# Block 0 of a fused retention and MLP kernel: who casts the first k and scales the first q, and which PSUM banks and which place four of its tiles have

## The chip, the cores and the metric

The kernel runs on one core of a Trainium2 chip. TensorE (PE) does the matrix products, VectorE (DVE), ScalarE (ACT) and GpSimd (POOL) the elementwise work, and SyncE (SP) issues most DMAs. The time is the device time of one execution in microseconds. The lower it is, the better.

## The reference, cut to what matters

```python
def _attn_ref(q, k, v):            # 4 batches, 8 heads, 768 steps, 64 wide
    gamma = 1.0 - 2.0 ** (-5.0 - np.arange(H))
    for t in range(S):
        state = gamma * state + outer(k[t], v[t])
        y[t] = scale * q[t] @ state

def _moe_ref(x, w_in, w_out):      # x: y as 3072 rows of 512; w_in 512 x 2048
    h = x @ w_in
    g = h * tanh(softplus(h))      # Mish
    return g @ w_out               # 2048 x 512
```

A decayed linear attention (retention) gives x, and a two-layer MLP with the Mish function follows. Inputs and output are float32.

## The kernel before

**Chunks and blocks.** The 24 chunks of 128 steps (6 for each batch) are worked off in blocks: block 0 holds four chunks (512 rows), the ten others two each. In a chunk the retention is a masked product of scores with v (the present part) plus q times a state of the chunks before (the past part). A block's y, transposed and rounded to fp16, is `xt`, the moving operand of the first MLP layer. Later blocks use Strassen-like seven products for both layers (`g1_seven`, `seven`); block 0 computes its first layer plainly, in 16 tiles u of 128 hidden features by 512 rows: `first_g1` for u = 0 to 3, in two halves of 256 rows (s = 0 for chunks 0 and 1, s = 1 for chunks 2 and 3), and `g1` for u = 4 to 15. Each tile is four matmuls over the 512 inputs (one half: four of 256 columns) and ends in `mish`, a ScalarE activation from PSUM.

**The order is written out.** The program states the order by hand, and each engine takes its instructions in that order; semaphores come from the data and the buffers. The function with the order of block 0 is `first_block`, followed by `first_g2` for the second layer.

**How block 0 starts.** `load_first_q` loads the q of all four chunks in two halves by heads, then k and v come in pairs of chunks (s = 0: chunks 0 and 1; s = 1: chunks 2 and 3), each in two halves of four heads (`load_two`), then the four slices of `w_in`, then those of `w_out`, all on SP's queue. `turn_first_q` scales one half of q to fp16 on VectorE (L255) and transposes it on PE (L261); `first_q_out` copies it out of PSUM. `cast_two` casts a half of k to fp16 on ScalarE (L286) or multiplies a half of v by its decay on GpSimd (L289); `turn_two` transposes k on PE (L300), and `turned_two` copies it out on ScalarE (L305). `scores_half` makes scores (L315), which VectorE masks in `mask_half` (L322). `outer_first` and `state_first` make the states (L334, L344, L346 on VectorE); `present_first` (L375) and `past_first` (L382) make y for two chunks in one PSUM tile, and `xt_out` copies both chunks to `xt` on ScalarE (L387). Here and there `spin` and `spin_wide` are matmuls on constants whose result nobody reads: they keep PE at work.

**Weights.** `cast_win` casts half a slice of `w_in` to fp16 (L212; L210 on ScalarE): slice 0 on GpSimd and VectorE, slices 1 and 2 on VectorE, slice 3 on ScalarE between two Mish. `cast_wout` does the same for `w_out` (L220 on VectorE, L223 on ScalarE). From these casts VectorE builds the sums for the later blocks (`win_sums`, L756; `weight_sums`, L708 to L711). In `first_g2`, PE's products (L1191) are copied out by ScalarE (L1197, and the snapshots L1200), then ScalarE casts its half of slice 2 of `w_out` (L223). GpSimd's `gate` (L428) makes it wait for `tmat`; behind it stand `cast_q` (L403) and `cast_v` (L420) of chunk 4, whose q and k PE then transposes in `turn` (L454).

**PSUM.** There are eight banks of 2 KB per partition. Pool `mmps` hands out four tiles of one bank in turn, pool `atps` two tiles of two banks in turn: scores, y, and later the outer products. A tile that is taken anew waits for the last reader of the tile that had its room.

Of the kernel before, what the change touches and what calls it, by code (L numbers as in the profile page):

```python
# [10 lines left out]
FP32 = mybir.dt.float32  # L11
AF = mybir.ActivationFunctionType
ALU = mybir.AluOpType
# [3 lines left out]
def kernel(  # L17
# [9 lines left out]
    nc = tc.nc  # L27
    B, H, S, D = q.shape
    d_model, d_ff = moe_w_in.shape
    P = 128  # L30
    C = 128
    NCH = S // C
    NCK = B * NCH
    HP = H // 2
    TB = 512
    CPB = TB // C
# [7 lines left out]
    FPS = NFB // NSL  # L44
# [10 lines left out]
    in_two = [vs_np[(jj % HB) * R + r] for r in range(R)]  # L55
    qvs_np = np.ascontiguousarray(np.concatenate([qs_np, vs_np, *spread, *in_two], 1))

    def toks(c):
        return slice(c * HB, (c + 1) * HB)
# [11 lines left out]
    op = ctx.enter_context(tc.tile_pool(name="rn_o", bufs=6))  # L71
# [10 lines left out]
    qs_spread = qvs[:, 2 * H:(2 + CPB) * H].rearrange("p (r h) -> p h r", r=CPB)  # L82
# [166 lines left out]
                q[0, a:a + H // 2, :TB].rearrange("h (p r) d -> p h r d", r=CPB))  # L249
        return qf  # L250

    def turn_first_q(qf, half):
        a, n = half * (H // 2), H // 2
        q16 = castp.tile([P, CPB, n, D], FP16, name="qfirst16", bufs=1, tag=f"qfirst16_{half}")
        nc.vector.tensor_tensor(  # L255
            q16.rearrange("p r h d -> p h r d"), qf[:, a:a + n],
            qs_spread[:, a:a + n].unsqueeze(3).broadcast_to((P, n, CPB, D)), op=ALU.mult)
        t_ps = mmps.tile([P, n // 2, CPB, P], FP16, name="t_ps", tag="mm")
        for i in range(n // 2):
            for r in range(CPB):  # L260
                nc.tensor.transpose(t_ps[:, i, r], q16[:, r, 2 * i:2 * i + 2], ident)  # L261
        return t_ps

    def first_q_out(half, t_ps, eng):
        n = HP // 2
        dst = qfirst_t[:, half * n:(half + 1) * n].rearrange("p i (t r) -> p i t r", r=CPB)
        src = t_ps.rearrange("p i r t -> p i t r")
        if eng is nc.scalar:
            nc.scalar.copy(dst, src)
        else:  # L270
            eng.tensor_copy(dst, src)
# [6 lines left out]
                "h (p r) d -> p h r d", r=R))  # L278
        raw[nm, s, half] = t

    def cast_two(nm, s, half):
        src = raw.pop((nm, s, half))
        if nm == "k":
            if s not in k16s:
                k16s[s] = castp.tile([P, 2, R, HP, D], FP16, name="qk16")
            nc.scalar.copy(k16s[s][:, half].rearrange("p r h d -> p h r d"), src)  # L286
        else:
            v16s[s, half] = castp.tile([P, R, HP, D], FP16, name="v16")
            nc.gpsimd.tensor_tensor(  # L289
                v16s[s, half].rearrange("p r h d -> p h r d"), src,  # L290
                vs_two[:, half * HP:(half + 1) * HP].unsqueeze(3).broadcast_to((P, HP, R, D)),
                op=ALU.mult)

    def turn_two(s, half):
        if s not in kts:
            kts[s] = qktp.tile([P, HP, R, P], FP16, name="qkt", bufs=4)
        t_ps = mmps.tile([P, HP // 2, R, P], FP16, name="t_ps", tag="mm")
        for j in range(HP // 2):
            for r in range(R):
                nc.tensor.transpose(t_ps[:, j, r], k16s[s][:, half, r, 2 * j:2 * j + 2], ident)  # L300
        t16s[s, half] = t_ps

    def turned_two(s, half):
        n = HP // 2
        nc.scalar.copy(kts[s][:, half * n:(half + 1) * n], t16s.pop((s, half)))  # L305
# [63 lines left out]
    def present_first(s, y, pairs):  # L369
        for i in pairs:  # L370
            half, j = divmod(i, HP // 2)
            for r in range(R):
                for c in range(2):
                    for hh in range(2):
                        nc.tensor.matmul(  # L375
                            y[64 * hh:64 * hh + 64, c, i], v16s[s, half][toks(c), r, 2 * j + hh],
                            amf[s, half][toks(c), hh, j, r], start=i == 0 and r == 0,
                            stop=s == 0 and c == 0 and r == R - 1, skip_group_check=True)

    def past_first(g, y):  # L380
        for i in range(HP):
            nc.tensor.matmul(  # L382
                y[:, g % 2, i], states[g - 1][:, i], qfirst_t[:, i, g * C:(g + 1) * C],
                start=False, stop=True, skip_group_check=True)

    def xt_out(g, y):
        nc.scalar.copy(xts[0][:, g:g + 2], y)  # L387

    def room16(g):
        if g not in cast:  # L390
# [54 lines left out]
    def spin_wide(at, n):  # L445
        nc.tensor.matmul(
            at[:, 0].rearrange("p j r t -> p (j r) t")[:, :n], tri,
            tri.unsqueeze(1).broadcast_to((P, n, C)), start=True, stop=True)
# [217 lines left out]
    def g1(blk, u):  # L666
        nt = BLOCKS[blk] * C
        per = TB // nt
        h_ps = mmps.tile([P, per, nt], FP32, name="h_ps", tag="mm")
        for j in range(per):  # L670
            s, f = divmod(u * per + j, FPS)
            for bp in range(NBP):
                nc.tensor.matmul(  # L673
                    h_ps[:, j], win(s, f, bp), xt(blk, bp),
                    start=(bp == 0), stop=(bp == NBP - 1))
        mish(blk, u, h_ps)
# [361 lines left out]
    def first_g1(h_ps, u, s):  # L1038
        t = slice(s * TB // 2, (s + 1) * TB // 2)
        for bp in range(NBP):  # L1040
            nc.tensor.matmul(  # L1041
                h_ps[:, 0, t], win(0, u, bp), xts[0][:, 2 * s:2 * s + 2, bp],
                start=bp == 0, stop=bp == NBP - 1, skip_group_check=True)

    def first_block():
# [11 lines left out]
        spin_wide(at, HP)  # L1057
        spin(at, 8)
        tq = turn_first_q(qf, 0)
        spin_wide(at, 3)  # L1060
        first_q_out(0, tq, nc.scalar)
        tq = [tq, turn_first_q(qf, 1)]
        cast_two("k", 0, 0)
        turn_two(0, 0)
        first_q_out(1, tq[1], nc.vector)
        turned_two(0, 0)
        cast_two("k", 0, 1)
        spin_wide(at, 3)
        scores_half(0, 0, at)
        mask_half(0, 0, at)  # L1070
        turn_two(0, 1)
        turned_two(0, 1)
        for half in range(2):
            cast_two("v", 0, half)
        at = at_tile()
        spin_wide(at, 3)
        scores_half(0, 1, at)
        mask_half(0, 1, at)
        cast_two("k", 1, 0)
# [6 lines left out]
        scores_half(1, 0, at)  # L1086
        mask_half(1, 0, at)
        y = atps.tile([P, 2, HP, C], FP32, name="y_ps", tag="at")
        present_first(0, y, range(HP))
        turn_two(1, 1)  # L1090
        turned_two(1, 1)
        state_first(1)
        past_first(1, y)
        xt_out(0, y)
        for half in range(2):
            cast_two("v", 1, half)
# [1 line left out]
        at = at_tile()  # L1098
        scores_half(1, 1, at)
        mask_half(1, 1, at)  # L1100
        y = atps.tile([P, 2, HP, C], FP32, name="y_ps", tag="at")
        outer_first(1, [0])
        state_first(2)
        h_ps = [mmps.tile([P, 1, TB], FP32, name="h_ps", tag="mm") for _ in range(2)]
        present_first(1, y, range(HP))
        past_first(2, y)
        past_first(3, y)
        xt_out(2, y)
        cast_win(0, 1, nc.vector)
        for u in range(FPS):  # L1110
            if u >= 2:
                h_ps.append(mmps.tile([P, 1, TB], FP32, name="h_ps", tag="mm"))
            first_g1(h_ps[u], u, 0)
        for u in range(FPS):
            first_g1(h_ps[u], u, 1)
# [280 lines left out]
```

## Time and profile before

| | |
|---|---|
| Runs before | 191.96, 193.19, 194.15 us; median 193.19 |
| Profiled execution | 192.43 us, its span 190.2 us |
| PE busy | 183.4 us, 96% of the span |
| VectorE, ScalarE, GpSimd busy | 155.3 us (82%), 127.7 (67%), 93.6 (49%) |
| Granted TensorE clock, mean | 0.997 |
| DMA | 36.17 MB, mean 190 GB/s |

A row of the trace in order of time reads: start in us from the span's start, us, engine, line, operation, output <- input, shapes, count, and in brackets how long the engine had been idle before it and what ended that wait. SPq and POOLq are issues of DMAs, PEld the loading of weights into PE. A row of the chain reads: start, us, engine, tile, line, count. A row of a stretch has its limits, its length, then for PE, PEld, DVE, ACT and POOL the busy us and the instructions, then the granted clock, the DMA's busy share and GB/s.

### The profile page before, as it was taken

Reading aid. Unit: us, or ns where it says so; the run is one execution under the profiler, and the core shown is the slowest. Engines: PE = TensorE matmul, PEld = TensorE weight load, DVE = VectorE, ACT = ScalarE, POOL = GpSimd, SP = SyncE. Lnnn points to the kernel's source line nnn. Section 1 sums busy time; section 2 is a strip of 40 time slices with the busy share of each in tenths; the row PEclk is TensorE's granted clock in tenths of the full one; section 3 lists DMA queues with packets and bytes.
Section 4 is the critical chain, followed back from the end, with each engine's and each line's share of the span. In section 5 each row is a group of like instructions: output and inputs, shape, how many; then the busy total and the mean of one; then the engine's idle time right before and its main releaser. Section 6 shows DMA issues by size and latency. Waiting matters only on the chain.

```text
span 190.2 us, 7745 instructions
## 1 busy us (share of the span) xinstructions
PE 183.4 (96%) x3298; PEld 156.1 (82%) x3298; DVE 155.3 (82%) x327; ACT 127.7 (67%) x246; POOL 93.6 (49%) x134
## 2 busy tenths in 40 slices
PE   6889999999999999999999999999999999999992
PEld 2457546885988988988988988988988989989981
DVE  3786799989899698797897897797897897796672
ACT  3564699463893893894794883883983974975960
POOL 6270206596777937933943934925925923000000
PEclk9999999999999999999999999999999999999998
DMA  5999999997999999999996996999997954300203
GB/s 164 351 369 406 404 408 259 293 263 77 193 190 264 197 258 245 158 207 173 139 206 160 173 164 193 192 116 172 177 177 152 142 163 60 114 3 6 107 0 110
DMA packets 95521, 36.17 MB, mean 190 GB/s; under 512 B 82560, under 2 KB 88960, under 8 KB 95488
## 3 DMA queue, kind: packets, MB, share of 16 engines
q1 hardware_dynamic: 74112, 32.78, 73.0%
q0 software_dynamic: 21088, 2.62, 21.6%
q8 instruction: 25, 0.41, 0.9%
q10 hardware_dynamic: 288, 0.30, 0.4%
q14 instruction: 8, 0.07, 0.1%
HBM read 27.30 MB, written 6.29 MB: 177 GB/s over the span
## 4 chain that ended last, share of the span: by engine, by line
PE 86%; DMA 5%; DVE 3%; ACT 1%; POOL 1%; issue 1%; DVEq 0%
PE o_ps L940 31%; PE h_ps L804 30%; PE h_ps L673 6%; PE o_ps L1191 5%; DMA qkt<-qk 3%; DMA qfirst<-in_q_dram 2%; PE o_ps L1251 2%; PE h_ps L1041 2%; PE y_ps L531 2%; PE at L498 2%; PE u_ps L484 2%; PE y_ps L542 1%; DVE am L322 1%; POOL qk L415 1%; DVE st L346 1%
## 5 line engine op out<-in xcount | busy, mean ns | idle before, releaser
L824 DVE TENSOR_TENSOR hsum<-h_ps,hsnap 128x512 f32<-128x512 f32 x60 | 38.7, 685 | 9.6 <-ACT hsnap L814 6.5
L814 ACT COPY hsnap<-h_ps 128x512 f32<-128x512 f32 x60 | 32.1, 589 | 9.9 <-PE h_ps L804 9.7
L804 PEld LDWEIGHTS <-wsum 128*128 128x128 f16 x640 | 36.2, 98 | 0.1
L819 ACT ACTIVATE g<-hsum 128x512 f16<-128x512 f32 x60 | 34.7, 642 | 0.5
L940 PEld LDWEIGHTS <-gsum 128*128 128x128 f16 x320 | 30.5, 98 | 3.7
L804 PE MATMUL h_ps<-xsum,wsum 128*128 128x128 f16 x480 | 30.1, 219 | 0.0
L940 PE MATMUL o_ps<-tmat,gsum 128*128 128x256 f16 x240 | 29.5, 273 | 0.0
L804 PEld LDWEIGHTS <-win 128*128 128x128 f16 x480 | 28.2, 98 | 0.9
L415 POOL DMA_DIRECT2D qk<-in_k_dram x36 | 27.6, 775 | 0.0
L940 PEld LDWEIGHTS <-g 128*128 128x128 f16 x248 | 22.7, 98 | 2.6
L403 POOL TENSOR_TENSOR qk<-qf,qvs 128x512 f16<-128x512 f32 x20 | 21.5, 1074 | 0.0
L420 POOL TENSOR_TENSOR v<-vf,qvs 128x512 f16<-128x512 f32 x20 | 21.1, 1077 | 0.0
L940 PE MATMUL o_ps<-wout,g 128*128 128x256 f16 (+1 forms) x168 | 20.8, 267 | 0.0
L804 PE MATMUL h_ps<-xt,win 128*128 128x128 f16 x320 | 19.6, 219 | 0.0
L549 ACT COPY hsum<-y_ps 128x512 f32<-128x512 f32 x9 | 5.3, 585 | 18.7 <-PE y_ps L542 16.3
L592 POOL TENSOR_TENSOR stc<-suc,gcv 128x256 f16<-128x256 f32 x15 | 9.9, 660 | 15.9 <-DVE suc L587 15.9
L961 DVE TENSOR_TENSOR osb<-o_ps,snap 128x256 f32<-128x256 f32 (+1 forms) x32 | 13.0, 413 | 4.8 <-PE o_ps L940 2.4
L949 ACT COPY snap<-o_ps 128x256 f32<-128x256 f32 x31 | 11.4, 371 | 5.5 <-PE o_ps L940 5.3
L428 POOL COPY gate<-gsum 128x1 f16<-128x1 f16 x10 | 1.9, 186 | 26.7 <-DVE gsum L911 26.7
L804 PE MATMUL h_ps<-xsum,win 128*128 128x128 f16 x160 | 12.3, 220 | 0.0
L804 PE MATMUL h_ps<-xt,wsum 128*128 128x128 f16 x160 | 12.2, 219 | 0.0
L819 ACT ACTIVATE g<-h_ps 128x512 f16<-128x512 f32 x20 | 12.0, 598 | 0.0
(138 smaller groups left out, 308.1 us busy)
## 6 DMA issues: line engine op xcount, KB each, us to landing
vf<-in_v_dram SPq DMA_DIRECT2D x24, 256.0 KB, 6.2
out_dram<-osb SPq DMA_DIRECT2D x22, 256.0 KB, 3.0
qf<-in_q_dram SPq DMA_DIRECT2D x20, 256.0 KB, 5.4
wi<-in_moe_w_in_dram SPq DMA_DIRECT2D x3, 1024.0 KB, 10.6
wt<-in_moe_w_out_dram SPq DMA_DIRECT2D x3, 1024.0 KB, 9.1
qk<-in_k_dram POOLq DMA_DIRECT2D x36, 64.0 KB, 4.7
qfirst<-in_q_dram SPq DMA_DIRECT2D x2, 512.0 KB, 4.3
kf<-in_k_dram SPq DMA_DIRECT2D x4, 256.0 KB, 5.0
```

Of the source, the lines that this page charges most:

```text
L403: nc.gpsimd.tensor_tensor(by_head(g, room16(g)[0]), by_head(0, loaded[g][0]), f.broadcast_to((P, 2, HP, D)), op=ALU.mult)
L415: nc.gpsimd.dma_start(room16(g)[1][:, x::2], src[:, HP * x:HP * x + HP])
L420: nc.gpsimd.tensor_tensor(room16(g)[2], loaded[g][2], vs.unsqueeze(2).broadcast_to((P, H, D)), op=ALU.mult)
L592: by.tensor_tensor(stcs[g], sus.pop(g), decay, op=ALU.mult)
L673: nc.tensor.matmul(h_ps[:, j], win(s, f, bp), xt(blk, bp), start=(bp == 0), stop=(bp == NBP - 1))
L804: nc.tensor.matmul(h_ps[g][:, f], w(g, f, d), x(d), start=first and f == 0 and d == 0, stop=d == n - 1, skip_group_check=True)
L814: nc.scalar.copy(x, h_ps)
L819: nc.scalar.activation(gt[:, fb:fb + FPS, j * P:(j + 1) * P], h, AF.Mish, scale=inv_boost3)
L824: nc.vector.tensor_tensor(h, h_ps, x, op=ALU.add)
L940: nc.tensor.matmul(t, x(f), w(f)[:, c], start=first and f == 0, stop=f == n - 1, skip_group_check=True)
L949: nc.scalar.copy(x[:, c], t)
L961: nc.vector.tensor_tensor(dst[:, c], t, plus[:, c], op=ALU.add)
```

## The change

1. `turn_first_q(qf, 1, True)`: of the second half of q, VectorE scales the first two heads and GpSimd the last two, a quarter of q.
2. The two halves of k of chunks 0 and 1 are cast by VectorE instead of ScalarE, right behind the scaling and ahead of the copy-out of q (`first_q_out(1)`); both are transposed and copied out before the first scores. On ScalarE two casts go, and the copies of both `kts` halves follow each other.
3. Three calls `spin_wide(at, 3)` become `spin_wide(at, 1)`.
4. y of chunks 2 and 3 is made in two `atps` tiles, of which each uses one bank, instead of one. `first_g1` of tiles 0 and 1 for s = 0 stands ahead of it.
5. `xt_out_by_two` copies chunk 2 on ScalarE and chunk 3 on VectorE, the latter behind `cast_win(0, 1)`.
6. `g1` of tiles 8 and 9 (`u // 2 == FPS`) takes its PSUM from `atps`, the pool of the scores, instead of `mmps`.

SP's order of instructions stays; GpSimd's order has one instruction more, ahead of the first v. PE has the same instructions apart from the width of three fillers.

```diff
--- before.py
+++ after.py
@@ -249,12 +249,15 @@
                 q[0, a:a + H // 2, :TB].rearrange("h (p r) d -> p h r d", r=CPB))
         return qf
 
-    def turn_first_q(qf, half):
+    def turn_first_q(qf, half, shared=False):
         a, n = half * (H // 2), H // 2
         q16 = castp.tile([P, CPB, n, D], FP16, name="qfirst16", bufs=1, tag=f"qfirst16_{half}")
-        nc.vector.tensor_tensor(
-            q16.rearrange("p r h d -> p h r d"), qf[:, a:a + n],
-            qs_spread[:, a:a + n].unsqueeze(3).broadcast_to((P, n, CPB, D)), op=ALU.mult)
+        m = n // 2 if shared else n
+        for b in range(0, n, m):
+            (nc.gpsimd if b else nc.vector).tensor_tensor(
+                q16[:, :, b:b + m].rearrange("p r h d -> p h r d"), qf[:, a + b:a + b + m],
+                qs_spread[:, a + b:a + b + m].unsqueeze(3).broadcast_to((P, m, CPB, D)),
+                op=ALU.mult)
         t_ps = mmps.tile([P, n // 2, CPB, P], FP16, name="t_ps", tag="mm")
         for i in range(n // 2):
             for r in range(CPB):
@@ -278,12 +281,16 @@
                 "h (p r) d -> p h r d", r=R))
         raw[nm, s, half] = t
 
-    def cast_two(nm, s, half):
+    def cast_two(nm, s, half, by_vector=False):
         src = raw.pop((nm, s, half))
         if nm == "k":
             if s not in k16s:
                 k16s[s] = castp.tile([P, 2, R, HP, D], FP16, name="qk16")
-            nc.scalar.copy(k16s[s][:, half].rearrange("p r h d -> p h r d"), src)
+            dst = k16s[s][:, half].rearrange("p r h d -> p h r d")
+            if by_vector:
+                nc.vector.tensor_copy(dst, src)
+            else:
+                nc.scalar.copy(dst, src)
         else:
             v16s[s, half] = castp.tile([P, R, HP, D], FP16, name="v16")
             nc.gpsimd.tensor_tensor(
@@ -373,18 +380,22 @@
                 for c in range(2):
                     for hh in range(2):
                         nc.tensor.matmul(
-                            y[64 * hh:64 * hh + 64, c, i], v16s[s, half][toks(c), r, 2 * j + hh],
+                            y[c][64 * hh:64 * hh + 64, i], v16s[s, half][toks(c), r, 2 * j + hh],
                             amf[s, half][toks(c), hh, j, r], start=i == 0 and r == 0,
                             stop=s == 0 and c == 0 and r == R - 1, skip_group_check=True)
 
     def past_first(g, y):
         for i in range(HP):
             nc.tensor.matmul(
-                y[:, g % 2, i], states[g - 1][:, i], qfirst_t[:, i, g * C:(g + 1) * C],
+                y[g % 2][:, i], states[g - 1][:, i], qfirst_t[:, i, g * C:(g + 1) * C],
                 start=False, stop=True, skip_group_check=True)
 
     def xt_out(g, y):
         nc.scalar.copy(xts[0][:, g:g + 2], y)
+
+    def xt_out_by_two(g, y):
+        nc.scalar.copy(xts[0][:, g], y[0])
+        nc.vector.tensor_copy(xts[0][:, g + 1], y[1])
 
     def room16(g):
         if g not in cast:
@@ -666,7 +677,10 @@
     def g1(blk, u):
         nt = BLOCKS[blk] * C
         per = TB // nt
-        h_ps = mmps.tile([P, per, nt], FP32, name="h_ps", tag="mm")
+        if u // 2 == FPS:
+            h_ps = atps.tile([P, 2, per, nt], FP32, name="h_ps", tag="at")[:, 0]
+        else:
+            h_ps = mmps.tile([P, per, nt], FP32, name="h_ps", tag="mm")
         for j in range(per):
             s, f = divmod(u * per + j, FPS)
             for bp in range(NBP):
@@ -1057,23 +1071,23 @@
         spin_wide(at, HP)
         spin(at, 8)
         tq = turn_first_q(qf, 0)
-        spin_wide(at, 3)
+        spin_wide(at, 1)
         first_q_out(0, tq, nc.scalar)
-        tq = [tq, turn_first_q(qf, 1)]
-        cast_two("k", 0, 0)
+        tq = [tq, turn_first_q(qf, 1, True)]
+        cast_two("k", 0, 0, True)
         turn_two(0, 0)
+        turned_two(0, 0)
+        cast_two("k", 0, 1, True)
+        turn_two(0, 1)
         first_q_out(1, tq[1], nc.vector)
-        turned_two(0, 0)
-        cast_two("k", 0, 1)
-        spin_wide(at, 3)
+        turned_two(0, 1)
+        spin_wide(at, 1)
         scores_half(0, 0, at)
         mask_half(0, 0, at)
-        turn_two(0, 1)
-        turned_two(0, 1)
         for half in range(2):
             cast_two("v", 0, half)
         at = at_tile()
-        spin_wide(at, 3)
+        spin_wide(at, 1)
         scores_half(0, 1, at)
         mask_half(0, 1, at)
         cast_two("k", 1, 0)
@@ -1086,11 +1100,12 @@
         scores_half(1, 0, at)
         mask_half(1, 0, at)
         y = atps.tile([P, 2, HP, C], FP32, name="y_ps", tag="at")
-        present_first(0, y, range(HP))
+        in_two = [y[:, c] for c in range(2)]
+        present_first(0, in_two, range(HP))
         turn_two(1, 1)
         turned_two(1, 1)
         state_first(1)
-        past_first(1, y)
+        past_first(1, in_two)
         xt_out(0, y)
         for half in range(2):
             cast_two("v", 1, half)
@@ -1098,18 +1113,19 @@
         at = at_tile()
         scores_half(1, 1, at)
         mask_half(1, 1, at)
-        y = atps.tile([P, 2, HP, C], FP32, name="y_ps", tag="at")
+        y = [atps.tile([P, 2, HP, C], FP32, name="y_ps", tag="at")[:, 0] for _ in range(2)]
         outer_first(1, [0])
         state_first(2)
         h_ps = [mmps.tile([P, 1, TB], FP32, name="h_ps", tag="mm") for _ in range(2)]
+        for u in range(2):
+            first_g1(h_ps[u], u, 0)
         present_first(1, y, range(HP))
         past_first(2, y)
         past_first(3, y)
-        xt_out(2, y)
         cast_win(0, 1, nc.vector)
-        for u in range(FPS):
-            if u >= 2:
-                h_ps.append(mmps.tile([P, 1, TB], FP32, name="h_ps", tag="mm"))
+        xt_out_by_two(2, y)
+        for u in range(2, FPS):
+            h_ps.append(mmps.tile([P, 1, TB], FP32, name="h_ps", tag="mm"))
             first_g1(h_ps[u], u, 0)
         for u in range(FPS):
             first_g1(h_ps[u], u, 1)
```

## The prediction

> **What bounds the kernel now.** I read the page first: one engine is busy nearly all the time.
>
> ```profile
> span 190.2 us, 7745 instructions
> PE 183.4 (96%) x3298; PEld 156.1 (82%) x3298; DVE 155.3 (82%) x327; ACT 127.7 (67%) x246; POOL 93.6 (49%) x134
> ```
>
> The profiled execution took 192.43 us, 2.2 more than its span, and the three runs have a median of 193.19 (191.96 to 194.15). PE is idle for 6.8 us in all. The stretches of equal work show where the idle time lies, and it is the stretch that the change edits:
>
> ```profile
> 0.00:17.00 17.00, 13.92 (x211) 7.88 (x212) 12.17 (x37) 7.83 (x12) 8.34 (x20) 1.00 0.95 312
> 17.00:31.00 14.00, 14.00 (x97) 7.90 (x95) 11.16 (x25) 11.28 (x19) 3.10 (x3) 1.00 1.07 396
> ```
>
> In the first 17 us PE is busy for 13.92 (3.08 idle, and part of the rest is `spin_wide`, which computes nothing); after it PE has no gap. The chain that ended last then stays on PE:
>
> ```profile
> 17.10 3.49 PE h_ps L1041 x32
> 20.59 0.37 PE u_ps L355 x16
> 20.96 10.53 PE h_ps L673 x48
> 31.50 6.11 PE o_ps L1191 x56
> ```
>
> Read alone, this says that whatever the prologue saves comes off the end. But a chain names one path. So I looked at what else could end at 37.5, in ScalarE's order of time and in the DMA of 3 to 31 us:
>
> ```profile
> DMA packets 10624, 10.75 MB, mean 384 GB/s; under 512 B 1486, under 2 KB 7552, under 8 KB 10621
> ...
> 18.73 1.30 DVE L212 CAST win<-wi 128x1024 f16<-128x1024 f32 x2 [1.48 <-DMA wi<-in_moe_w_in_dram]
> ...
> 24.00 1.04 ACT L210 CAST win<-wi 128x1024 f16<-128x1024 f32 x1 [0.57 <-DMA wi<-in_moe_w_in_dram]
> 24.95 0.59 ACT L689 ACTIVATE g<-h_ps 128x512 f16<-128x512 f32 x1
> 25.43 1.04 ACT L210 CAST win<-wi 128x1024 f16<-128x1024 f32 x1
> 26.37 1.08 ACT L689 ACTIVATE g<-h_ps 128x512 f16<-128x512 f32 x2
> 27.34 0.63 ACT L223 CAST wout<-wt 128x512 f16<-128x512 f32 x1
> 27.84 2.08 ACT L689 ACTIVATE g<-h_ps 128x512 f16<-128x512 f32 x4
> 29.76 1.09 ACT L223 CAST wout<-wt 128x1024 f16<-128x1024 f32 x1
> 30.70 1.63 ACT L689 ACTIVATE g<-h_ps 128x512 f16<-128x512 f32 x3
> ...
> 32.41 0.45 ACT L1197 COPY osb<-o_ps 128x256 f32<-128x256 f32 x1
> ...
> 32.84 0.37 ACT L1200 COPY snap<-o_ps 128x256 f32<-128x256 f32 x1
> 33.28 0.37 ACT L1200 COPY snap<-o_ps 128x256 f32<-128x256 f32 x1
> 33.55 1.05 ACT L223 CAST wout<-wt 128x1024 f16<-128x1024 f32 x1
> ```
>
> The queues deliver 384 GB/s without a pause (10.75 MB in 28 us). At 24.00 ScalarE waits for the last slice of `w_in` to land, and from there it has no gap until the cast of `wout` at 33.55: each row begins before the one above has ended. What hangs on that cast:
>
> ```profile
> 32.21 1.04 PE L1191 MATMUL o_ps<-tmat,gsum 128*128 128x256 f16 x8
> ...
> 34.63 0.69 DVE L709 TENSOR_TENSOR tmat<-wout,tmat 128x1024 f16<-128x1024 f16 x1 [0.30 <-ACT wout L223]
> ...
> 35.47 0.50 POOL L428 COPY gate<-tmat 128x1 f16<-128x1 f16 x1 [3.54 <-DVE tmat L709]
> ...
> 35.84 0.68 DVE L1164 TENSOR_TENSOR gsum<-g,gsum 128x1024 f16<-128x1024 f16 x1
> 35.93 1.50 POOL L403 TENSOR_TENSOR qk<-qf,qvs 128x512 f16<-128x512 f32 x1
> ...
> 37.48 0.23 PEld L454 LDWEIGHTS <-qk 128*128 128x128 f16 x4 [0.15 <-POOL qk L403]
> ```
>
> VectorE's `tmat` waits 0.30 for that cast, GpSimd's gate for `tmat`, the scaling of q for the gate, and PE's transposes at 37.48 wait 0.15 for the q. So a second chain, from the DMA over ScalarE, VectorE and GpSimd, arrives at PE together with PE's own work. The change shortens PE's side alone.
>
> **The change part by part.** The prologue's rows:
>
> ```profile
> 4.69 2.58 DVE L255 TENSOR_TENSOR qfirst<-qfirst,qvs 128x1024 f16<-128x1024 f32 x2 [1.81 <-DMA qfirst<-in_q_dram]
> 7.33 0.62 PE L261 MATMUL t_ps<-ident,qfirst 128*128 128x128 f16 x8
> 7.99 1.23 DVE L271 COPY qfirst_t<-t_ps 128x1024 f16<-128x1024 f16 x1 [0.72 <-PE t_ps L261]
> 8.40 2.08 POOL L289 TENSOR_TENSOR v<-vf,qvs 128x512 f16<-128x512 f32 x2 [4.22 <-DMA vf<-in_v_dram]
> 9.24 0.53 ACT qk L286
> 9.83 1.23 DVE L322 TENSOR_TENSOR am<-at,tri_first 128x1024 f16<-128x1024 f32 x1 [0.62 <-PE at L315]
> 13.51 1.04 POOL L212 CAST win<-wi 128x1024 f16<-128x1024 f32 x1
> 15.97 0.68 DVE L346 TENSOR_TENSOR st<-u_ps,gcm 128x512 f16<-128x512 f32 x1
> 16.56 0.69 DVE L212 CAST win<-wi 128x1024 f16<-128x1024 f32 x1
> 17.14 1.01 ACT L387 CAST xt<-y_ps 128x1024 f16<-128x1024 f32 x1 [1.93 <-PE y_ps L382]
> ```
>
> *The quarter of q.* VectorE's two scalings run 4.69 to 7.27. Now the second is half as long (2.58/4 = 0.65, from 5.97), and GpSimd, idle until 8.40, scales the rest: a 128x512 multiply by `qvs`, 2.08/2 = 1.04 in the row of `v`. Beside each other they end at 7.1, and the second transposes (7.33 before) come 0.2 earlier. Bounds: 1.50 is what L403, of the same size, takes where VectorE's L1164, with two inputs from SBUF as well, runs into it, which gives 7.5; one after the other, 0.65 + 1.04, gives 7.7, 0.4 later. I take 7.4, nearer to L403, because here too VectorE reads two tensors beside it.
>
> The Trainium skill (SBUF — State Buffer, Who interferes with whom) says that a VectorE instruction with two SBUF inputs and a GpSimd instruction that reads SBUF shut each other out for the whole instruction. By it the two quarters would run one after the other and end at 7.7; the 1.50 of L403 agrees in sign.
>
> *The first k casts.* They leave ScalarE, where each holds 0.53 of the chain between two evacuations of `kts`. On VectorE one costs between half of the 0.69 of L212 and that 0.53; I take 0.4. If a slice of k lands late, L271 and the first mask wait behind its cast. They stand ahead of the copy-out L271, in the time in which VectorE waits for the transposes, so the first mask follows transposes 0.62 and copy 1.23: 7.4 + 0.62 + 1.23 = 9.25, against 9.83. With the bounds above, and the k transposes behind a late q (0.3 more at the late end), 9.0 to 9.9. From there VectorE alone needs four masks of 1.23 and three states of 0.68, 6.96 us, and before it took 9.83 to 16.65, 6.82 with overlap. So the last state ends 0 to 0.8 earlier; I take 0.3, because GpSimd's `win` cast, 13.51 to 14.55, stands behind multiplies of v that wait for landings (as the row of 8.40 does) and does not move.
>
> *Two tiles ahead of y.* Eight of the 32 matmuls of L1041 go ahead: 8 x 3.49/32 = 0.87 us. They run after 14.55, while the last mask is still on VectorE, so this comes off the path behind y. The second y tile now takes the bank of the last scores, so all of `present_first` waits for the last mask, not its second half; the moved matmuls cover that. If that cover were gone, it would cost part of the 0.87 that it covers.
>
> *xt by two.* 1.01 on ScalarE becomes half there, half on VectorE behind the `win` cast, which ends at 17.25 and now holds up tile 2. Behind VectorE's half wait the casts of the next `w_in`, which land only at 18.73: cost nothing.
>
> Stage sum: tile 2 starts between 16.95 and 17.25 and 24 matmuls follow (24 x 0.109 = 2.62), so L355 begins at 19.6 to 19.9 instead of 20.59. **Gain of the stage: 0.7 to 1.0 us.** ScalarE's wait at 24.00 grows by about as much.
>
> *Tiles 8 and 9 on the scores' banks.* Those banks are free after xt, so tiles 10 to 13 find theirs read long before. Tiles 14 and 15 still reuse those of 10 and 11, as before. SP's order does not change, nor do its DMAs.
>
> *What is left at 37.5.* The landing at 24.00 stays, since the queues were full since 3 us; ScalarE's ten microseconds of work behind it stay; the last Mish ends at 32.33. PE's early arrival can only help the two snapshots, which wait for PE's row at 32.21. Work on ScalarE follows a copy of this size by 0.27 (33.28 to 33.55), so the first could start at 32.68 behind the copy of 32.41, and the second at 32.95. The second also needs the bank that the last Mish frees: 32.33 + 4 x 0.109 + 0.17 (the tail by which 1.04 is more than 8 x 0.109) = 32.94. Then the cast begins at 33.22, not 33.55. **Sum: 0.3 us**, handed on to `tmat`, gate, q and PE. Bounds: 0 if the snapshots stay, 0.33 if both follow at once. 192.43 - 0.3 = 192.1 on the profiled execution; on the median 193.19 - 0.3 = **192.9**.
>
> **The rivals.** A: PE is what bounds. Then the stage's 0.7 to 1.0 passes whole: 192.2 to 192.5. For it, the chain on PE and the 0.15 and 0.30 waits, small enough to be noise of one execution; against it, ten microseconds of ScalarE without a gap behind a landing.
>
> B: the prologue gives much more and it passes, up to all 3.08 of PE's idle time: 190.1, and halfway between A and that 191.15. For it: the shorter fillers free PE too. Against it: the landings, and VectorE's 6.96.
>
> C, the other side: the clock. Three fillers of 384 columns become 128. These rows show what a slow clock costs:
>
> ```profile
> 1.88 3.44 PE L446 MATMUL at<-tri 128*128 128x512 f32 x4 [1.88 <-POOL tri L96]
> 6.43 0.86 PE L446 MATMUL at<-tri 128*128 128x384 f32 x2
> ```
>
> Per column the first fillers take 0.86/512 = 1.68 ns, the later ones 0.43/384 = 1.12, two thirds. PE worked from 1.88 to about 5 before it was fast. If the clock falls in the thinner stretch and stays low through L1041, its 3.49 run twice as long: 193.19 + 3.49 - 0.7 = 196.0. A fall that is mended after 3 us of work costs 1.5: 194.0. It decides, against a 1% line, from a loss of 0.7 + 1.93 = 2.6 on. For it: PE then has less filler in every pause of 5 to 11 us. Against it: the longest thing that PE waits for there is a VectorE row of 1.23.
>
> The Trainium skill (TensorE: Matmul & The Clock Gate, Part 1) halves the clock only after an idle window of about 3.4 us; by that rule C doesn't happen.
>
> That the change doesn't do what it says (the quarter so late that the prologue stays) gives 193.2, inside the forecast's range.
>
> **How the numbers follow.** Forecast 0.58, A 0.17, B 0.12, C 0.13. A measurement of this kernel can tell about 1%, 1.93 us, from no change. B passes that in two cases of three (0.08), and the spread of the three runs (2.2 us, 1.1%) puts 0.04 of the others there: faster 0.12. C passes it in somewhat over half (0.08), the spread adds 0.02: slower 0.10. Within 1%: 0.78. Range: the runs lie from 1.2 under to 1.0 over their median, which about 192.9 is 191.7 to 193.9; B at its halfway point and C's mended fall with some spread widen it to 191.2 and 194.5.
>
> **What would show it.** Right: the first mask at 9.0 to 9.9, L355 at 19.6 to 19.9, ScalarE's wait for `w_in` still ending at 24.0 with 1.2 to 1.6 idle before it, the `wout` cast at 33.2 to 33.5, the transposes of L454 within 0.4 of 37.48. Wrong: that landing earlier than 23.5, ScalarE with gaps between 24 and 33, L454 more than 0.6 earlier (A), or a granted clock under 1.00 in 5 to 20 us (C).

## The result and the profile after

The changed kernel takes 192.12 us (median of 22 runs, 191.35 to 193.19), the kernel before 192.72 (22 runs, 191.71 to 194.18). The ratio is 0.9959, 95% interval 0.994 to 0.9978: 0.4 to 1.2 us less. That is within the 1% that was forecast, in the forecast direction, and inside the range; 192.9 was 0.8 too high. Of that, 0.47 is the base (the three runs shown had a median of 193.19, the 22 have 192.72), and 0.3 is the size of the gain: 0.6 measured by the medians, 0.3 forecast. The forecast's bounds for the gain, 0 to 0.33, lie under the whole interval of 0.4 to 1.2.

The page of the changed kernel, in the two lines shown before, and the two stretches of the prologue (columns: stretch, its length, then busy time of PE, PEld, DVE, ACT, POOL, then the granted clock, DMA share and GB/s):

```profile
span 189.8 us, 7746 instructions
PE 183.3 (97%) x3298; PEld 156.9 (83%) x3298; DVE 156.7 (83%) x330; ACT 126.0 (66%) x244; POOL 94.7 (50%) x135
```

```profile
0.00:17.00 17.00, 14.21 (x216) 9.39 (x217) 13.26 (x39) 6.79 (x10) 9.81 (x21) 1.00 0.94 312
17.00:31.00 14.00, 14.00 (x97) 7.65 (x95) 12.18 (x26) 11.04 (x20) 3.26 (x4) 1.00 1.07 397
```

The span is 0.4 shorter (190.2 before). ScalarE has given about 1 us of the first 17 to VectorE; PE is again without a gap from 17 on, and so this view doesn't say where the 0.4 comes from. The chain that ended last is on PE again:

```profile
17.32 2.71 PE h_ps L1055 x24
20.02 0.37 PE u_ps L362 x16
20.39 10.47 PE h_ps L687 x48
30.86 6.29 PE o_ps L1207 x56
```

L362 is the L355 of before: it starts at 20.02 instead of 20.59, 0.57 earlier. The timeline puts both starts 0.07 earlier, and its starts are used from here on. In the kernel before, then in the changed one:

```profile
20.52 0.44 PE L355 MATMUL u_ps<-v,qk 64*64 64x64 f16 x16
```

```profile
19.95 0.44 PE L362 MATMUL u_ps<-v,qk 64*64 64x64 f16 x16
```

The timeline of the prologue:

```profile
4.69 2.02 DVE L257 TENSOR_TENSOR qfirst<-qfirst,qvs 128x1024 f16<-128x1024 f32 x2 [1.80 <-DMA qfirst<-in_q_dram]
6.14 1.49 POOL L257 TENSOR_TENSOR qfirst<-qfirst,qvs 128x512 f16<-128x512 f32 x1 [1.98 <-DMA qfirst<-in_q_dram]
6.29 1.06 PE L264 MATMUL t_ps<-ident,qfirst 128*128 128x128 f16 x8
6.77 1.47 DVE L291 CAST qk<-kf 128x512 f16<-128x512 f32 x2
7.15 0.74 PE L457 MATMUL at<-tri 128*128 128x128 f32 x2
7.68 0.77 PE L264 MATMUL t_ps<-ident,qfirst 128*128 128x128 f16 x8
9.89 2.35 DVE L329 TENSOR_TENSOR am<-at,tri_first 128x1024 f16<-128x1024 f32 x2 [0.17 <-PE at L322]
14.49 1.22 DVE L329 TENSOR_TENSOR am<-at,tri_first 128x1024 f16<-128x1024 f32 x1
15.15 1.04 PE L1055 MATMUL h_ps<-xt,win 128*128 128x256 f16 x8
15.63 0.68 DVE L353 TENSOR_TENSOR st<-u_ps,gcm 128x512 f16<-128x512 f32 x1
16.12 0.64 PE L382 MATMUL y_ps<-am,v 64*64 64x128 f16 x32
16.69 0.62 PE L389 MATMUL y_ps<-qfirst_t,st 128*128 128x128 f16 x8
17.35 0.69 DVE L398 CAST xt<-y_ps 128x512 f16<-128x512 f32 x1 [0.44 <-PE y_ps L389]
18.10 1.64 PEld L1055 LDWEIGHTS <-win 128*128 128x128 f16 x16 [0.19 <-DVE xt L398]
```

The first mask comes at 9.89, no earlier than before (9.83). In this execution PE was still slow at the first transposes: eight take 1.06, where the profile of before has

```profile
5.97 0.62 PE L261 MATMUL t_ps<-ident,qfirst 128*128 128x128 f16 x8 [0.23 <-DVE qfirst L255]
```

The two moved tiles run at 15.15, behind them y and the states, and of tiles 2 and 3 the weight loads wait 0.19 for VectorE's half of `xt`. From there to the transposes of chunk 4, the second chain:

```profile
23.80 1.05 ACT L210 CAST win<-wi 128x1024 f16<-128x1024 f32 x1 [0.95 <-DMA wi<-in_moe_w_in_dram]
32.46 0.75 ACT L1216 COPY snap<-o_ps 128x256 f32<-128x256 f32 x2
33.09 1.07 ACT L223 CAST wout<-wt 128x1024 f16<-128x1024 f32 x1
34.19 0.69 DVE L723 TENSOR_TENSOR tmat<-wout,tmat 128x1024 f16<-128x1024 f16 x1 [0.44 <-ACT wout L223]
35.03 0.50 POOL L439 COPY gate<-tmat 128x1 f16<-128x1 f16 x1 [3.69 <-DVE tmat L723]
35.49 1.50 POOL L414 TENSOR_TENSOR qk<-qf,qvs 128x512 f16<-128x512 f32 x1
37.04 0.23 PEld L465 LDWEIGHTS <-qk 128*128 128x128 f16 x4 [0.18 <-POOL qk L414]
```

ScalarE now waits 0.95 for the last slice of `w_in` (0.57 before), and the transposes come at 37.04 instead of 37.48. Of this 0.44 the landing itself is 0.20 (23.80 for 24.00), the snapshots the rest: the cast of `wout` follows the landing by 9.29 instead of 9.55. The 0.4 is what the span is shorter by.

On its way there PE itself is held up, at its first products of the second layer. In the changed kernel, then before (the second product of before, at 32.21, stands in the prediction):

```profile
30.69 1.12 PE L1207 MATMUL o_ps<-wout,g 128*128 128x256 f16 x8
31.70 1.08 PE L1207 MATMUL o_ps<-tmat,gsum 128*128 128x256 f16 x8
32.62 3.66 PE L1207 MATMUL o_ps<-wout,g 128*128 128x256 f16 x32
```

```profile
31.33 1.04 PE L1191 MATMUL o_ps<-wout,g 128*128 128x256 f16 x8
33.08 3.66 PE L1191 MATMUL o_ps<-wout,g 128*128 128x256 f16 x32
```

From the first product to the third it is 1.93 instead of 1.75, so PE loses 0.18 while ScalarE's last Mish run beside it (30.51 to 32.14). The rows name no releaser for so short a wait. That it hangs on ScalarE is borne out by e12 below; that it is the PSUM which the last Mish free, as the prediction had it for the second snapshot, is likely and not shown.

### The profile page after: what moved, and what is told of

Its sections match the earlier page's. It is cut to its first block, busy times and chain, and to the rows that moved or that the text cites. A ratio compares the mean times of both kernels' runs of the same rounds, so it can differ in the third digit from the quotient of the medians.

```text
span 189.8 us, 7746 instructions
## 1 busy us (share of the span) xinstructions
PE 183.3 (97%) x3298; PEld 156.9 (83%) x3298; DVE 156.7 (83%) x330; ACT 126.0 (66%) x244; POOL 94.7 (50%) x135
## 4 chain that ended last, share of the span: by engine, by line
PE 94%; DVE 3%; issue 1%; POOL 0%; ACT 0%; POOLq 0%; DVEq 0%
PE h_ps L818 34%; PE o_ps L954 32%; PE h_ps L687 6%; PE o_ps L1207 5%; PE at L457 2%; PE h_ps L1055 2%; PE o_ps L1267 2%; PE y_ps L542 2%; PE at L509 2%; PE u_ps L495 2%; DVE am L329 2%; PE y_ps L553 2%; PE t_ps L264 1%; DVE osb L975 1%; PE at L322 0%
## 5 line engine op out<-in xcount | busy, mean ns | idle before, releaser
L818 PE MATMUL h_ps<-xt,win 128*128 128x128 f16 x320 | 19.6, 219 | 0.0
```

Of the source, the lines that this page charges most:

```text
L818: nc.tensor.matmul(h_ps[g][:, f], w(g, f, d), x(d), start=first and f == 0 and d == 0, stop=d == n - 1, skip_group_check=True)
```

## The experiments

All ratios are to the kernel before, run beside it on the same chip. The theory is that of the prediction, two chains that meet at the transposes of chunk 4: one of PE, one from the landing of the last `w_in` slice over ScalarE. The rival is A, PE alone. Each profile gives two intervals to the start of those transposes: from L362 (L355 before), and from ScalarE's first cast of the last slice. Worked out from the timeline rows of each kernel:

| kernel | L355/L362 starts | cast of `w_in` starts (its wait for DMA) | transposes | from L355/L362 | from the cast |
|---|---|---|---|---|---|
| before | 20.52 | 24.00 (0.57) | 37.48 | 16.96 | 13.48 |
| after | 19.95 | 23.80 (0.95) | 37.04 | 17.09 | 13.24 |
| e1 front alone | 20.32 | 24.28 (1.06) | 37.77 | 17.45 | 13.49 |
| e2 back alone | 20.73 | 24.27 (0.63) | 37.62 | 16.89 | 13.35 |
| e3 after + PE work | 20.42 | 23.93 (0.60) | 37.31 | 16.89 | 13.38 |
| e4 before + PE work | 21.83 | 24.64 (none) | 38.72 | 16.89 | 14.08 |
| e5 after, slice not loaded | 20.66 | 23.46 (none) | 37.55 | 16.89 | 14.09 |
| e6 before, slice not loaded | 21.03 | 23.83 (none) | 37.91 | 16.88 | 14.08 |
| e9 after, no quarter | 19.87 | 23.84 (1.06) | 37.08 | 17.21 | 13.24 |
| e10 before, no first fillers | 22.67 | 25.47 (none) | 39.56 | 16.89 | 14.09 |
| e11 after, no first fillers | 20.81 | 24.39 (0.67) | 37.70 | 16.89 | 13.31 |

Two floors stand out: 16.89 when PE's chain ends last, 13.24 when the landing's does. The transposes start at the later of L362 + 16.89 and cast + 13.24, within 0.07, in every row but e1. The floors are read off these same rows, 13.24 off two of them, so this is a description that fits and no independent proof. The two aren't separate to the end, either: PE's products are held up beside ScalarE's last Mish (the 0.18 above), and ScalarE's snapshots wait for PE's products. e7, e8 and e12 aren't in the table, since their edits change the work between the cast and the transposes.

**e1: the front alone.** Before, with the changed order up to the scores (quarter, k casts, narrow fillers), and y, `xt` and the tiles as before:

```
-        spin_wide(at, 3)
+        spin_wide(at, 1)
-        tq = [tq, turn_first_q(qf, 1)]
-        cast_two("k", 0, 0)
+        tq = [tq, turn_first_q(qf, 1, True)]
+        cast_two("k", 0, 0, True)
...
```

> The kernel before with parts 1 to 3 alone: the shared scaling of q, the k casts on VectorE, the narrow fillers. Two chains (the forecast): the first mask does not come earlier than about 9.8, because GpSimd's quarter takes 1.49 and the copy-out still stands behind it, so nothing reaches the end: 0 to -0.2 us. PE bounds (rival A) with a gain from the front: -0.3 to -0.6 us and the transposes of chunk 4 as much earlier than 37.48.

Measured 192.51 against 192.94, ratio 0.9969 (0.9942 to 0.9996). PE in the timeline of e1:

```profile
20.69 6.22 PE L680 MATMUL h_ps<-xt,win 128*128 128x512 f16 x28
27.31 4.48 PE L680 MATMUL h_ps<-xt,win 128*128 128x512 f16 x20 [0.40 <-ACT g L696]
```

PE comes early (20.32), ScalarE's Mish are held up behind the landing at 24.28, and after seven tiles PE waits 0.40 for one of them to free a bank. The copies behind it start later, and neither floor is reached. The changed kernel has no such wait, nor has e9, in which PE is as far ahead of the landing (19.87 to 23.84; here 20.32 to 24.28): in both, tiles 8 and 9 have banks of their own. The prediction had costed that edit at nothing; it is what lets PE run on while ScalarE waits for the landing.

**e2: the back alone.** The changed kernel with the front of before (the diff of e1 the other way round).

> The change without its front: parts 4 to 6 alone (tiles 0 and 1 ahead of y, xt by two, tiles 8 and 9 on the scores' banks). Two chains: these parts alone give the stage its gain, L362 at about 20.0 and the whole -0.3 to -0.6 us of the change. Rival, the parts need each other: under half of it, and L362 later than 20.3.

Measured 192.79 against 192.94, ratio 0.9978 (0.9948 to 1.0008). L362 at 20.73 and the 16.89 show PE's chain ending last. About half of the gain, not the whole: the expectation of 20.0 for L362 was wrong. The intervals of e1, e2 and the changed kernel overlap, so how the gain splits between front and back isn't settled; that either half alone brings all of it isn't borne out.

**e3 and e4: 0.44 us more work for PE,** half of tile 0 a second time, ahead of the second halves, in the changed kernel and in the one before:

```
+        first_g1(h_ps[0], 0, 0)
         for u in range(FPS):
```

> The changed kernel with the first half of tile 0 computed a second time ahead of the second halves: 4 matmuls of 256 columns, 0.44 us of PE work that leaves the result as it is. Two chains: PE is ahead of ScalarE by about 0.3 to 0.4, so at most 0.1 to 0.2 us of the 0.44 arrives at the transposes of chunk 4 (37.05 to 37.25) and the time stays 0.2 to 0.5 under the kernel before. PE bounds: all 0.44 arrives, the transposes at 37.5, the time that of the kernel before.

> The kernel before with the same 0.44 us of PE work in the same place. Two chains: PE was on time there within 0.0 to 0.3, so 0.3 to 0.45 us arrive and the kernel is that much slower than before, the transposes of chunk 4 at 37.8 to 37.95. ScalarE alone bounds already before: under 0.15.

In the changed kernel it costs nothing that shows: 192.08, ratio 0.9954 (0.9927 to 0.9982), beside 0.9959 without it; all of the 0.44 would be 0.9982, the very end of the interval. In the one before it costs 0.54 by the ratio, 1.0028 (1.0 to 1.0056, so 0 to 1.1 us): 193.33. ScalarE's first cast of the last slice in e3, then the same in e4 with the Mish ahead of it:

```profile
23.93 1.04 ACT L210 CAST win<-wi 128x1024 f16<-128x1024 f32 x1 [0.60 <-DMA wi<-in_moe_w_in_dram]
```

```profile
24.14 0.60 ACT L689 ACTIVATE g<-h_ps 128x512 f16<-128x512 f32 x1 [0.27 <-PE h_ps L673]
24.64 1.04 ACT L210 CAST win<-wi 128x1024 f16<-128x1024 f32 x1
```

In e3 ScalarE still waits for DMA; in e4 it doesn't, it waits for PE. So the runs speak against rival A in the changed kernel and for it in the one before; neither interval alone decides it. The theory as the prediction put it took both kernels to be held by the landing.

**e5 and e6: the landing taken away.** The last slice of `w_in` is not loaded, slice 2 is cast in its place:

```
             t = wstage.tile([P, NBP, TB], FP32, name="wi", tag="wt", bufs=4)
+            if s == NSL - 1:
+                wtmps[which, s] = wtmps[which, s - 1]
+                return
```

> The changed kernel without the load of the last slice of w_in (1 MB): ScalarE casts the third slice a second time in its place, so nothing waits for that landing. Two chains: ScalarE begins the cast right behind the Mish of tile 5, at about 22.8 instead of 23.8, without a wait; ScalarE's chain moves up by that, PE's order bounds, and the transposes of chunk 4 come at 36.4 to 36.8. If that landing did not bound: 37.0 to 37.1, and the time that of the changed kernel, -0.3 to -0.8 to before.

> The kernel before, also without the load of the last slice of w_in. Two chains: here PE is the later one already, so the landing gives little: transposes of chunk 4 at 37.2 to 37.4 where the clock is up by 5 us, the time 0 to 0.3 under before; the difference to the changed kernel without that load is the stage's own gain, 0.5 to 0.9, more than the 0.3 of the forecast. If the landing bounds both alike, both gain the same, 0.5 or more.

Measured: e5 192.46, ratio 0.9976 (0.995 to 1.0001); e6 193.2, ratio 1.0014 (0.999 to 1.0038). The cast no longer waits in either (the table), and both reach the transposes on PE's floor. They differ by 0.74 us, as expected of PE's own earliness. But neither is faster than its version with the load: something is lost 18 us later. PE's weight loads in the second block, in e5:

```profile
55.96 0.21 PEld L512 LDWEIGHTS <-qkt 64*64 64x64 f16 x16 [0.88 <-DMA qkt<-qk]
```

PE waits 0.88 for a transposing DMA that the profiles of before and after don't make it wait for, and 0.70 in e6. From the transposes of chunk 4 to the end of the span it is 153.5 in both, 152.7 and 152.8 in the profiles of before and after, and 152.4 to 153.1 in all the others. So these two runs don't tell by the time what the landing costs. e5's first q also landed a microsecond later than in the profile of after (VectorE's first scaling starts at 5.71, not 4.69), so its 37.55 isn't what the landing alone is worth.

**e7 and e8: half of the last slice cast by GpSimd,** to shorten ScalarE's work behind the landing:

```
-                7: [(cast_win, NSL - 1, 1, nc.scalar), (more_sums,)],
+                7: [(cast_win, NSL - 1, 1, nc.gpsimd), (more_sums,)],
```

> The changed kernel with the second half of the last slice of w_in cast by GpSimd, which is idle from 22.5 to 28.8, instead of ScalarE (1.04 us off ScalarE's chain behind the landing). Two chains: ScalarE's chain ends up to 0.9 earlier, PE bounds again, transposes of chunk 4 at 36.5 to 36.8, the time 0.2 to 0.6 under the changed kernel (0.8 to 1.4 under before). Against it: GpSimd's cast (1.04 alone) beside VectorE's sums with two inputs from SBUF may stretch to 2 and hold those up: then no gain, or a loss of 0.3.

> The kernel before with the same cast on GpSimd. Two chains: PE is late there itself, so at most 0.1 to 0.3 under before. If ScalarE alone bounds both kernels: 0.5 to 0.9 under before, as much as in the changed kernel.

Neither gains: e7 192.93, ratio 0.9988 (0.9958 to 1.0018), 0.3% more than the changed kernel, though the intervals overlap; e8 193.85, ratio 1.0037 (1.001 to 1.0064), slower than before. The transposes come at 38.88 and 39.09. PE and ScalarE of e7:

```profile
33.58 1.05 PE L1207 MATMUL o_ps<-tmat,gsum 128*128 128x256 f16 x8 [0.34 <-DVE gsum L1174]
34.22 0.81 ACT L1216 COPY snap<-o_ps 128x256 f32<-128x256 f32 x2 [0.57 <-PE o_ps L1207]
34.93 1.05 ACT L223 CAST wout<-wt 128x1024 f16<-128x1024 f32 x1
```

ScalarE now waits 0.57 for PE's product, PE 0.34 for a sum by VectorE. The work behind the landing hangs on three engines, and freeing one of them moves the wait to another. e8 shows that for the kernel before 0.1 to 0.3 less was the wrong sign.

**e9: no quarter on GpSimd.** VectorE scales all of q:

```
-        tq = [tq, turn_first_q(qf, 1, True)]
+        tq = [tq, turn_first_q(qf, 1)]
```

> The changed kernel with the whole second half of q scaled by VectorE (1.22 us there), as before the change; GpSimd has no part in it. If the two engines shut each other out (GpSimd's quarter then took 1.49 where v's multiply takes 1.04), the scaling ends 1.25 behind the landing of that half instead of 1.6, and the first mask comes 0.1 to 0.35 earlier behind it than in the changed kernel (3.58 to 3.9); the time stays that of the changed kernel within 0.2, since ScalarE's chain bounds. If the quarter helps: first mask 0.3 later, time the same or up to 0.3 more.

Measured 192.3 against 193.04, ratio 0.9976 (0.995 to 1.0002), not to be told from the changed kernel. The front of e9:

```profile
5.18 2.50 DVE L257 TENSOR_TENSOR qfirst<-qfirst,qvs 128x1024 f16<-128x1024 f32 x2 [2.29 <-DMA qfirst<-in_q_dram]
7.59 0.85 DVE L291 CAST qk<-kf 128x512 f16<-128x512 f32 x2
9.79 2.36 DVE L329 TENSOR_TENSOR am<-at,tri_first 128x1024 f16<-128x1024 f32 x2 [0.18 <-PE at L322]
```

VectorE's start to the first mask takes 4.61 (5.18 to 9.79); in e3, with the quarter on GpSimd and PE as fast at the first transposes (0.62), it takes 4.84 (5.17 to 10.01). Other profiles agree: 4.62 in e12, also without the quarter, 4.84 to 4.89 in e1, e5 and e7 with it. So the quarter costs 0.2 at the front rather than saving any: GpSimd takes 1.49 for it, and VectorE's two k casts beside it 1.41 to 1.48 instead of 0.85. At 37.08 (13.24 behind the cast) none of this shows: the landing ends last.

**e10 and e11: without the first fillers,** so that PE gets fast late, in the kernel before and in the changed one:

```
         at = at_tile()
-        spin_wide(at, HP)
-        spin_wide(at, HP)
-        spin(at, 8)
```

> The kernel before without the first fillers (two of 4x128 columns in float32 and two on the identity), so that the clock comes up later than 8 us. If the phase of the clock is what makes the kernel before slower on average than its first profile: first mask 0.5 to 1.0 later behind the landing of q (4.3 to 4.8, against 3.8), and since PE is on time there, the time 0.3 to 1.0 over before. If the clock doesn't matter there: within 0.2.

> The changed kernel without the first fillers. Two chains: the same loss at the first mask, but PE is ahead by 0.2 to 0.6, so the time is only 0 to 0.4 over the changed kernel, still under before. If PE bounds, it loses as much as the kernel before does.

Measured: e10 194.29, ratio 1.0066 (1.0036 to 1.0095), 1.3 us lost; e11 192.54, ratio 0.9978 (0.9955 to 1.0001), 0.4 us more than the changed kernel, within the intervals. PE at the front of e10, then of e11:

```profile
7.28 1.59 PE L446 MATMUL at<-tri 128*128 128x384 f32 x2
8.66 1.06 PE L261 MATMUL t_ps<-ident,qfirst 128*128 128x128 f16 x8
9.94 1.59 PE L446 MATMUL at<-tri 128*128 128x384 f32 x2
```

```profile
7.29 0.74 PE L457 MATMUL at<-tri 128*128 128x128 f32 x2
7.82 1.06 PE L264 MATMUL t_ps<-ident,qfirst 128*128 128x128 f16 x8
```

While PE is slow, a filler of 384 columns stands for 1.59 in the way of the second transposes, one of 128 for 0.74. The first mask comes at 12.15 in e10 (later than expected) and at 10.75 in e11. So, against what rival C feared, the changed kernel is less sensitive to a slow PE, and by these rows narrow fillers are a part of that; how large a part isn't shown, since the rest of its front differs too, and its wait for the landing hides some of what PE loses.

**e12: less on ScalarE,** an attempt at a better version: no quarter, the first half slice of `wout` all on VectorE, and one sum of g moved behind the next late ones:

```
-        tq = [tq, turn_first_q(qf, 1, True)]
+        tq = [tq, turn_first_q(qf, 1)]
...
-                9: [(cast_wout, 0, 1), (room_for_more,), (bring_first,)],
+                9: [(cast_wout, 0), (room_for_more,), (bring_first,)],
...
-                13: [(cast_wout, 1, 2), (room_for_more,), (g_sum, 2), (g_sum, 3)],
+                13: [(cast_wout, 1, 2), (room_for_more,), (g_sum, 2)],
...
         some_late(1)
+        g_sum(3)
```

> The changed kernel with both chains shortened: no quarter on GpSimd (as the run above), ScalarE's part of the cast of slice 0 of w_out given to VectorE (0.5 us off ScalarE between the landing and the last Mish), and one of VectorE's sums (g_sum 3) moved behind the tmat for which GpSimd's gate waits. Two chains: the last Mish of block 0 begins 0.5 earlier behind the landing, transposes of chunk 4 0.2 to 0.5 earlier than in the changed kernel, the time 0.2 to 0.5 under it. If ScalarE's chain is not what bounds: the same as the changed kernel, or 0.2 more for VectorE's longer cast.

Measured 192.72 against 193.04, ratio 0.9992 (0.9964 to 1.0021): not faster than the changed kernel. The first transposes do come earlier, at 36.85 (cast + 13.05; PE's floor of 19.91 + 16.89 is 36.80): with half a microsecond less on ScalarE, PE's first product of the second layer starts at 30.65 and the third at 32.45, 1.80 apart instead of 1.93, and most of PE's wait there is gone. The next transposes come later, 39.76 instead of 39.59. Between them, in e12:

```profile
35.82 1.53 DVE L1180 TENSOR_TENSOR gsum<-g,gsum 128x1024 f16<-128x1024 f16 x1
37.27 1.53 DVE L725 TENSOR_TENSOR tmat<-wout,tmat 128x1024 f16<-128x1024 f16 x1
38.22 1.49 POOL L414 TENSOR_TENSOR qk<-qf,qvs 128x512 f16<-128x512 f32 x1
39.76 0.40 PE L465 MATMUL t_ps<-ident,qk 128*128 128x128 f16 x4 [0.29 <-POOL qk L414]
```

VectorE's sums now run beside GpSimd's next scaling, which takes 1.49 (1.04 in the profile of after), and what was won is lost by the next transposes. That is 0.17; why the median is 0.6 higher than the changed kernel's isn't settled.

## Why the prediction was right, and where it was off

**What held.** The changed kernel is capped by the landing of the last `w_in` slice: ScalarE's wait ends at 23.80, the transposes follow by 13.24 there and in e9, and 0.44 us more work on PE costs nothing that shows (e3; in that profile PE's floor is 0.14 over the landing's, less than the interval can tell). Of the 0.20 by which PE's own floor is missed there, 0.18 is lost in the products beside ScalarE's last Mish, and in e12, with less on ScalarE, most of that is gone. By the floors, PE's 0.57 would otherwise have passed nearly whole: 36.84 is 19.95 + 16.89. The snapshots did follow the copies at once, and the cast of `wout` came at 33.09; put 0.20 later for the landing, that is 33.29, inside 33.2 to 33.5. The granted clock is 1.00 in the stretches above, and behind 9 us no row is slow: scores of the same shape take 0.42 before and after. C did not happen, and e10 and e11 speak for the narrow fillers, not against them. B did not happen either: halfway to it the gain would have been 2.0, and the interval ends at 1.2. The Trainium skill (TensorE: Matmul & The Clock Gate, Part 1) has the clock fall only behind an idle window of about 3.4 us; the trace agrees as far as it goes: behind the first transposes PE waits for nothing longer than 0.32.

**How much the number says.** Little: the range of 191.2 to 194.5 holds the forecast, A and no change alike. From the median of the 22 runs before, the forecast gives 192.4 and A's 0.7 to 1.0 gives 191.7 to 192.0; 192.12 lies between them. Of the five signs that were to show it right, only the first mask came as stated; L362 (19.95), ScalarE's wait (0.95), the `wout` cast (33.09) and the transposes (0.44 from 37.48, 0.4 allowed) were missed, most of them narrowly. So it is no credit to the mechanism that the time lies in the range; under A it would have as well.

**The term that was mis-sized** is the sum's 0.3. It was the difference of two chains in one execution of the kernel before, and that execution was a favourable one for PE. Its own profile already sat on PE's floor: 20.52 + 16.89 is 37.41, and 37.48 was seen; the landing alone would have allowed 24.00 + 13.24, 37.24. In other executions of the same prologue PE is later: L355 at 21.03 (e6), 21.44 (e8) and 21.39 (e4 less its 0.44). With 16.89 behind them, the four average 37.99. For the changed kernel the later of the two floors is 37.04 in its own profile, 37.17 in e3 (by the landing, the extra 0.44 left out), 37.55 in e5 (PE) and 38.20 in e7 (a landing as late as 24.96), 37.49 on average. So means over executions make some 0.5 of it, against 0.3 forecast and 0.6 measured; four executions each, of kernels that differ elsewhere (e5 and e6 have no landing at all), don't fix it better. The step that failed is the one that took the 24.00 for the bound of the kernel before, because it stood in its profile: there PE was the bound, within 0.07 even in the execution profiled, and e4 agrees, with 0.54 lost for 0.44 added.

**What moves PE from one execution to the next** is seen in two rows: when q lands (VectorE's first scaling starts at 4.69 to 5.71 in the profiles here), and how long PE stays slow. Eight transposes of q take 0.62 in the profile of before, 1.03 in that of e8, of the same prologue:

```profile
6.48 1.03 PE L261 MATMUL t_ps<-ident,qfirst 128*128 128x128 f16 x8
8.36 0.61 PE L261 MATMUL t_ps<-ident,qfirst 128*128 128x128 f16 x8
```

There the first mask comes at 10.75. In the profile of after PE was slow too (1.06), and the mask still came at 9.89. Counted from VectorE's first scaling, the mask follows by 5.14 in before and e6, where PE was fast, and by 5.53 and 5.56 in e4 and e8, where it was slow; in the changed order it follows by 4.84 to 4.89 (e1, e3, e5, e7) and by 5.20 in the profile of after. So the two profiles side by side, one with a fast PE and one with a slow one, showed no gain at the front where like with like shows 0.3 or more. L355 goes the same way: 15.83 behind the first scaling in before and e6, 16.21 (less the 0.44) and 16.25 in e4 and e8; in the changed kernel 15.26 with the slow PE, 14.81 to 15.34 with a fast one (e3 less its 0.44, e5, e7).

**By the steps.** *The quarter* was to end at 7.4; it began at 6.14, took 1.49 and ended at 7.63. The row of L403 (1.50), which was the bound, would have given the duration; 7.7 was the end by the Trainium skill (SBUF — State Buffer, Who interferes with whom), whose rule of a shared port agrees in sign and nearly in size: the quarter ends 0.92 behind the end of VectorE's scaling (6.71), and a multiply of this size takes 1.04 alone. That the two k casts (1.47, taken 0.8) would be stretched too was missed, and so was that the quarter costs 0.2 at the front (e9) instead of saving it. *The first mask* at 9.89 lies at the late end of 9.0 to 9.9. *The last state* ends at 16.31, 0.34 earlier (taken 0.3). *The two tiles* were to run while the mask is still on VectorE. They run 15.15 to 16.19, and the last mask ends at 15.71: y starts at 16.12, 0.4 behind the mask, and the past part at 16.69, 0.38 behind the state. So they don't only fill the wait for the mask, they outlast it, and y waits for them. *`xt` by two* was costed at nothing; tiles 2 and 3 wait 0.19 for VectorE's half, which ends at 18.04. Tile 2 starts at 17.15, as forecast, and without these 0.19 L362 would have come at 19.76, inside 19.6 to 19.9. *The stage* gave 0.57 between the two profiles and not 0.7 to 1.0, but that sets a fast PE before against a slow one after; like with like it is 0.5 to 1.0 by the numbers above, about as forecast. *ScalarE's wait* grew to 0.95, not 1.2 to 1.6, because of the 0.57 and with the landing 0.20 earlier. *Tiles 8 and 9* were costed at nothing; e1 shows 0.40 where they lack banks of their own.

## What to carry to other kernels

Where two chains meet, write down for each the shortest interval from its own last free event to the meeting point (here 16.89 from PE's start of the stage, 13.24 from the landing); several profiles give these floors, and then the time of any execution is the later of two sums. A gain is the mean of that maximum over executions and not its value in the one profiled: an edit that shortens the chain that varies can be worth more than a profile with that chain on time shows (here some 0.5 against 0.3, from four executions each). One profile is one draw: before two are set side by side, compare the rows that vary by themselves, here the landing of q and the first transposes. Work pulled ahead of a wait is free only until that wait ends, and a buffer that lets an engine run on while another waits for memory is part of the gain, not a detail.

## What the runs showed of the hardware

- The granted clock reads 1.00 over 4 to 10 us in all of these profiles, and yet eight transposes of the same shape take 0.62 or 1.06 there. Within one kernel's prologue that differs from execution to execution; the rows' durations show it, the clock column doesn't. The Trainium skill (TensorE: Matmul & The Clock Gate, Part 1) has the first matmuls slow for about 3.4 us of work and the phase of that vary from run to run; the rows agree in kind.
- GpSimd and VectorE stretch each other, and with casts of one input from SBUF as well: 1.49 for GpSimd's 128x512 scaling (1.04 alone), 1.41 to 1.48 for two k casts (0.85 alone), 1.53 for a 128x1024 sum in fp16 (0.69 alone).
- The same load lands at different times: ScalarE's wait for the last slice of `w_in` ends at 23.80 (after) to 24.96 (e7), with SP's order the same. Most of that is a shift of the whole stream: the first q is there at 4.69 in the one and 5.63 in the other.
